# Pairwise maxima of a top-32 search by a one-source reduction, and a planner with new costs

## The chip, the cores and the metric

One core of one Trainium2 chip. The metric is the device time of one execution in microseconds (us), the median of several runs. Engines are called as in the profile: PE (TensorE matmul), PEld (its weight load), DVE (VectorE), ACT (ScalarE), POOL (GpSimd), SP (SyncE, which here only issues DMAs).

## What is computed

Inputs q, k, v are 8 batches x 8 heads x 576 tokens x 64 in f32. For each head the scores are q times k transposed over 8; of each row of 576 scores only the 32 largest stay, a softmax runs over these, and the result is multiplied by v. The eight heads are put side by side (4608 tokens x 512) and go through two matrices, with a squared ReLU between.

```python
scores = scale * np.matmul(q, k.transpose(0, 1, 3, 2))
kth = np.partition(scores, -top_k, axis=-1)[..., -top_k:-top_k + 1]
mask = scores >= kth
...
attn = attn / (np.sum(attn, axis=-1, keepdims=True) + 1e-09)
...
h = x @ w_in
r = np.maximum(h, 0.0)
g = r * r
return (g @ w_out).astype(np.float32)
```

## The kernel before, in words

**Work items.** A head pair has 9 blocks of 128 query rows: four for each head, and one that holds the last 64 rows of both. With 32 head pairs that makes 288 items, and an item is a tile `s` of 128 rows x 576 scores. `top_k` (L426 and on) takes them in groups of two, the fourth group of each head pair in threes: 128 groups.

**The search for the 32nd largest.** DVE's MAX8 gives the 8 largest values of a row, and MATCH_REPLACE8 (with a short MATCH_VALUE_LOAD ahead of it) overwrites them; four rounds give 32. To shorten the rows, `top_k` first folds them. Line by line, for one item:

- L522, DVE: `m` (288 wide) is the elementwise maximum of the two halves of `s`. L521, POOL, through the helper `whole` (its instructions have the line L514): `t1` is the sum of the two halves taken as int32; the smaller of the two is got back later by a subtraction.
- L528, DVE: `pp` (144 wide) is the maximum of the two halves of `m`: the maximum of four scores, here called the quad maximum. L527, POOL: `t2` is the int32 sum of the halves of `m`.
- L531, POOL: the part `mid` of `f`, `t2 - pp`. L534, POOL: the part `low` of `f`, `t1 - m`.
- L539 to L550, DVE: MAX8 of `pp`, replace, MAX8 and replace over 144 columns, then over 288 (which needs `mid`); L553, DVE: the last MAX8 over all 576 (which needs `low`) gives `kth`.

In the trace the names are `m`, `pp`, `f`, `a`, `c` and `kth`, and `t` stands for both `t1` and `t2` (288 and 144 wide). The groups' lists are built so that an operation is given for all items of a group before the next operation. There are two buffers of `t1` and of `t2`, and four of `m`, `pp` and `f`.

**Around it.** PE makes the scores in PSUM, ACT copies them to `s` (L458). After `kth`, ACT makes the mask `w` (L561). `attend` (L577 and on) has PE make the transposed scores with the mask, ACT the exponentials, PE the product with v; DVE takes a reciprocal of the row sums (L661), whose source is one column out of each 65 of `av`, and POOL scales by it (L663). `feed` (L683) runs the two matrices on PE, with ACT's ReLU and square; in the last two batches POOL (L717) or DVE (L714) squares.

**The order of the work.** Nothing is ordered by hand. `Plan.op` (L89) records each operation with an engine, a duration `dur` in us, a due time `prio`, what it reads and writes, and the tiles that it takes from pools. `Plan.schedule` (L117) plays these durations through: whenever an engine is free, it starts the ready operation with the earliest due time whose tiles can be had. The order that comes out for each engine is the program of that engine; it is fixed, and on the chip semaphores alone hold an instruction back. So a duration in the source changes no instruction, but can change the order of all of them, on all five engines and on SP's DMA queue. The planner knows of no resource that two engines share. `Pool.find` (L38) picks the slots: PSUM has 8 banks, and tiles of width 2 take an even pair, the one that has been in the list of free slots longest. No tile has a width of 3.

The planned cost of an operation is written where it is recorded: for one item L522 .42, L528 .27, POOL's four .81, .46, .48 and .88; MAX8 .215, .365 and .665 for 144, 288 and 576 columns.

A second program (`again`, with `full` true) is there for the case that the folded search missed a value; a flag decides, and it doesn't run here.

Of the kernel before, what the change touches and what calls it, by code (L numbers as in the profile page):

```python
# [5 lines left out]
ALU = mybir.AluOpType  # L6
# [14 lines left out]
class Pool:  # L21
# [16 lines left out]
    def find(self, width):  # L38
        if width == 1:
            if not self.free:  # L40
                return None
            if self.name == "psum":
                half = [s for s in self.free if (s ^ 1) not in self.free]
                s = half[0] if half else self.free[0]
            else:
                s = self.free[0]
            self.free.remove(s)
            return s
        for s in self.free:
            if s % width == 0 and all(s + i in self.free for i in range(width)):  # L50
                for i in range(width):
                    self.free.remove(s + i)
                return s
        return None
# [21 lines left out]

class Op:
    __slots__ = ("eng", "dur", "prio", "fn", "deps", "tiles", "takes", "n", "users", "start", "end",
                 "idx", "sem", "val", "ndma", "seq", "vc", "waits", "wars", "later", "nbf")


ENGS = ("pe", "act", "dve", "gp", "sp")
# [2 lines left out]
class Plan:  # L85
    def __init__(self):
        self.ops = []

    def op(self, eng, dur, prio, fn, r=(), w=(), u=(), hold=(), take=(), after=(), order=(), sem=None, ndma=0, nbf=0.0):  # L89


        o = Op()
        o.eng, o.dur, o.prio, o.fn = eng, dur, prio, fn
        o.sem, o.ndma, o.seq, o.nbf = sem, ndma, len(self.ops), nbf
        o.takes = list(take)
        o.users = []
        o.start = o.end = o.idx = o.val = o.vc = None
        deps = set(after)
        for t in r:
            deps.update(t.writers)  # L100
        for t in u:
            deps.update(t.ops)
        for t in list(r) + list(w) + list(u) + list(hold):
            t.ops.append(o)
            t.left += 1
        for t in list(w) + list(u):
            t.writers.append(o)
        for t in o.takes:
            t.taker = o
        o.later = ({t.taker for t in list(r) + list(w) + list(u) + list(hold)} | set(order)) - deps - {o, None}  # L110
        o.deps = deps
        o.wars = list(w) + list(u)
        o.tiles = list(r) + list(w) + list(u) + list(hold)
        self.ops.append(o)
        return o

    def schedule(self, t0=0.0, latency=0.12, own=0.07):  # L117

        left = {}
        for o in self.ops:  # L120
            left[o] = len(o.deps | o.later)
            for d in o.deps | o.later:
                d.users.append(o)
        ready = {e: [] for e in ENGS}
        busy = {e: t0 for e in ENGS}
        order = {e: [] for e in ENGS}
        events = []
        n = 0

        def push(t, kind, x):  # L130
            nonlocal n
            heapq.heappush(events, (t, n, kind, x))
            n += 1

        for o in self.ops:
            if left[o] == 0:
                push(max(t0, t0 + o.nbf), "ready", o)
        push(t0, "go", None)
        readyat = {o: t0 + o.nbf for o in self.ops}
        done = 0  # L140
        while events:
            t = events[0][0]
            while events and events[0][0] <= t + 1e-9:
                _, _, kind, x = heapq.heappop(events)
                if kind == "end":
                    done += 1
                    for tl in x.tiles:
                        tl.left -= 1
                        if tl.left == 0 and tl.slot is not None:
                            for i in range(tl.width):  # L150
                                tl.pool.last[tl.slot + i] = tl
                            tl.pool.give(tl.slot, tl.width)
                    for v in x.users:
                        left[v] -= 1
                        lat = own if v.eng == x.eng else latency
                        readyat[v] = max(readyat[v], t + lat)
                        if left[v] == 0:
                            push(readyat[v], "ready", v)
                elif kind == "ready":
                    heapq.heappush(ready[x.eng], (x.prio, x.seq, x))  # L160
            for e in ENGS:
                if busy[e] > t + 1e-9:
                    continue
                skipped = []
                while ready[e]:
                    item = heapq.heappop(ready[e])
                    o = item[2]
                    got = []
                    ok = True
                    for tl in o.takes:  # L170
                        s = tl.pool.take(tl)
                        if s is None:
                            ok = False
                            break
                        got.append((tl, s))
                    if not ok:
                        for tl, s in got:
                            tl.pool.undo(s, tl.width)
                        skipped.append(item)
                        continue  # L180
                    for tl, s in got:
                        tl.slot = s
                        tl.prev = []
                        for i in range(tl.width):
                            p = tl.pool.last[s + i]
                            if p is not None:
                                tl.prev.append(p)
                    o.start = t
                    hold = o.dur if e != "sp" else 0.6 * o.ndma
                    o.end = t + o.dur + (hold if e == "sp" else 0)  # L190
                    busy[e] = t + hold
                    order[e].append(o)
                    push(busy[e], "go", None)
                    push(o.end, "end", o)
                    break
                for item in skipped:
                    heapq.heappush(ready[e], item)
        assert done == len(self.ops), (done, len(self.ops), t, [
            (e, i[0], [(x.pool.name, len(x.pool.free)) for x in i[2].takes]) for e in ENGS for i in sorted(ready[e])[:4]])
        self.order = order  # L200
        return max(o.end for o in self.ops)
# [75 lines left out]
def bass_top_k_attn__then__act_relu_squared_kernel(  # L277
# [60 lines left out]
    def at(t):  # L338
        return mem[t.pool.name][t.slot]
# [25 lines left out]
    def build(full, weights, pl):  # L365
# [60 lines left out]
        def top_k(gi, qk, tg, dw):  # L426
# [41 lines left out]
            def dve(dur, fn, **kw):  # L468
                dk[0] += 1
                return pl.op("dve", dur, tg + .34 * dk[0], fn, **kw)  # L470
# [38 lines left out]
            else:  # L509
# [8 lines left out]
                for i in range(nb):  # L518
                    A, B = (lambda i=i: at(st[i])[:, 0:HALF]), (lambda i=i: at(st[i])[:, HALF:S])
                    M, L = (lambda i=i: at(m[i])[:, :]), (lambda i=i: at(t1[i])[:, :])  # L520
                    whole(.81, tg - 1, i, ALU.add, L, A, B, r=[st[i]], w=[t1[i]], take=[t1[i]])  # L521
                    dve(.42, lambda i=i, A=A, B=B: vec.tensor_tensor(at(m[i])[:, :], A(), B(), ALU.max),  # L522
                        r=[st[i]], w=[m[i]], take=[m[i]])
                for i in range(nb):
                    M1, M2 = (lambda i=i: at(m[i])[:, 0:QUART]), (lambda i=i: at(m[i])[:, QUART:HALF])
                    Q, L = (lambda i=i: at(pp[i])[:, :]), (lambda i=i: at(t2[i])[:, :])
                    whole(.46, tg - .5, i, ALU.add, L, M1, M2, r=[m[i]], w=[t2[i]], take=[t2[i]])  # L527
                    dve(.27, lambda i=i, M1=M1, M2=M2: vec.tensor_tensor(at(pp[i])[:, :], M1(), M2(), ALU.max),  # L528
                        r=[m[i]], w=[pp[i]], take=[pp[i], f[i]] + ([a] if i == 0 else []))
                for i in range(nb):  # L530
                    mid.append(whole(.48, tg + .5, i, ALU.subtract, lambda i=i: at(f[i])[:, QUART:HALF],  # L531
                                     lambda i=i: at(t2[i])[:, :], lambda i=i: at(pp[i])[:, :],
                                     r=[t2[i], pp[i]], w=[f[i]]))
                    low.append(whole(.88, tg + 2.5, i, ALU.subtract, lambda i=i: at(f[i])[:, HALF:S],  # L534
                                     lambda i=i: at(t1[i])[:, :], lambda i=i: at(m[i])[:, :],
                                     r=[t1[i], m[i]], w=[f[i]]))
                prev = [[] for _ in range(nb)]
# [379 lines left out]
```

## Time and profile before

| | |
|---|---|
| Median of three runs | 1082.91 us (1082.89 to 1084.41) |
| The profiled execution's own time | 1080.87 us |
| Its span in the trace | 1079.0 us |
| Granted TensorE clock, mean | 0.954 of full speed |
| Instructions | 23727 |

The span runs from the first to the last recorded instruction. "Busy" of a group is the time in which at least one of its instructions was under way, "mean ns of one" the mean length of one; since an engine begins an instruction shortly before the one ahead of it ends, means add up to more than the busy time. The idle time of an engine is put down to the semaphore event that ended it.

### The profile page before, as it was taken

What the parts mean: (1) busy time and instruction counts of PE and PEld (TensorE: products, weight loads), DVE (VectorE), ACT (ScalarE), POOL (GpSimd) and SP (SyncE); (2) the same over time, 40 slices, a digit from 0 to 9 for tenths busy, and PEclk for the clock granted to TensorE, in tenths of its full rate; (3) what the DMA queues carried; (4) which work ended last, traced back from release to release, by engine and by line L of the source; (5) the groups of instructions that cost most, each with busy time, mean ns of one, the idle gap of its engine ahead of it and who ended that gap; (6) DMA issues with size and microseconds to landing.
All of it is one profiled execution on the core that took longest, in us unless ns stands there. A gap on an engine that the chain in (4) does not pass through costs nothing.

```text
span 1079.0 us, 23727 instructions
## 1 busy us (share of the span) xinstructions
PE 918.1 (85%) x8035; PEld 548.5 (51%) x8082; DVE 980.8 (91%) x3538; ACT 765.9 (71%) x1341; POOL 906.7 (84%) x1391
## 2 busy tenths in 40 slices
PE   6766868788899998889888899898888998979897
PEld 4434435444555555545455445555455554644554
DVE  5999999599999999599999999799998899999951
ACT  5645658766698678867688777887688776656652
POOL 7998989689988898588897999789897799999871
PEclk9878789999999999999899999999999999898999
DMA  6533310220200112112110013001220100000001
GB/s 146 130 101 100 111 46 13 56 54 21 71 12 12 53 48 57 23 42 54 28 45 2 24 51 93 23 2 52 67 50 1 44 21 16 2 1 21 21 16 38
DMA packets 124419, 47.77 MB, mean 44 GB/s; under 512 B 116608, under 2 KB 116608, under 8 KB 124288
## 3 DMA queue, kind: packets, MB, share of 16 engines
q1 hardware_dynamic: 124288, 46.16, 16.6%
q8 instruction: 65, 1.06, 0.4%
q14 instruction: 66, 0.54, 0.2%
HBM read 36.70 MB, written 9.44 MB: 43 GB/s over the span
## 4 chain that ended last, share of the span: by engine, by line
DVE 59%; POOL 13%; PE 12%; issue 10%; ACT 5%; SPq 0%; DMA 0%; POOLq 0%; DVEq 0%
DVE kth L553 15%; PE ps L360 12%; DVE c L547 11%; DVE m L522 10%; DVE f L550 8%; POOL f L514 7%; DVE pp L528 7%; POOL t L514 5%; DVE f L541 4%; DVE a L539 3%; ACT w L561 2%; ACT s L458 1%; POOL x L663 1%; PE ps L363 1%; DVE rzall L661 1%
## 5 line engine op out<-in xcount | busy, mean ns | idle before, releaser
L360 PE MATMUL ps<-qk 64*128 64x288 f32 (+7 forms) x2640 | 434.4, 443 | 60.7 <-ACT w L561 19.3
L561 ACT ACTIVATE w<-s,kth 128x576 bf16<-128x576 f32 x288 | 214.5, 771 | 137.3 <-DVE kth L553 136.9
L360 PEld LDWEIGHTS ps<-qk 64*128 64x128 f32 (+1 forms) x2640 | 216.4, 185 | 178.6 <-ACT w L561 33.3
L514 POOL TENSOR_TENSOR t<-s 128x288 int32<-128x288 int32 x288 | 234.0, 823 | 33.0 <-ACT s L458 30.5
L514 POOL TENSOR_TENSOR f<-t,m 128x288 int32<-128x288 int32 x288 | 228.1, 807 | 0.0
L514 POOL TENSOR_TENSOR t<-m 128x144 int32<-128x144 int32 x288 | 180.8, 638 | 49.9 <-DVE m L522 47.8
L550 DVE MATCH_REPLACE8 f<-c,f 128x144 f32<-128x144 f32 (+1 forms) x576 | 206.4, 363 | 0.0
L553 DVE MAX8 kth<-f 128x8 f32<-128x576 f32 x288 | 202.9, 742 | 2.6 <-POOL f L514 2.6
L620 ACT ACTIVATE p<-ps 128x640 bf16<-128x640 f32 (+1 forms) x192 | 155.2, 809 | 57.3 <-PE ps L360 56.0
L522 DVE TENSOR_TENSOR m<-s 128x288 f32<-128x288 f32 x288 | 158.8, 583 | 40.8 <-ACT s L458 40.8
L458 ACT COPY s<-ps 128x576 f32<-128x576 f32 x288 | 170.8, 642 | 33.2 <-PE ps L360 32.6
L547 DVE MAX8 c<-f 128x8 f32<-128x144 f32 (+1 forms) x576 | 190.8, 367 | 2.0 <-POOL f L514 1.9
L360 PE MATMUL ps<-wo,g 128*128 128x512 bf16 (+1 forms) x593 | 151.5, 383 | 8.7 <-ACT p L620 2.1
L360 PE MATMUL ps<-xt,win 128*128 128x288 bf16 (+2 forms) x1088 | 142.9, 284 | 7.4 <-ACT g L706 2.4
L514 POOL TENSOR_TENSOR f<-t,pp 128x144 int32<-128x144 int32 x288 | 141.7, 509 | 3.2 <-DVE pp L528 3.2
L360 PEld LDWEIGHTS ps<-steep_bf,w 128*128 128x128 bf16 (+1 forms) x1600 | 83.6, 102 | 110.4 <-issue 109.4
L528 DVE TENSOR_TENSOR pp<-m 128x144 f32<-128x144 f32 x288 | 131.5, 492 | 0.4
L360 PE MATMUL ps<-steep_bf,w 128*128 128x128 bf16 (+3 forms) x1600 | 124.0, 222 | 0.0
L360 PEld LDWEIGHTS ps<-xt,win 128*128 128x128 bf16 x1088 | 97.4, 99 | 40.0 <-ACT g L704 3.3
L360 PEld LDWEIGHTS ps<-wo,g 128*128 128x128 bf16 (+1 forms) x640 | 56.1, 101 | 60.7 <-issue 8.2
L541 DVE MATCH_REPLACE8 f<-a,pp 128x144 f32<-128x144 f32 x288 | 81.4, 287 | 0.0
L663 POOL TENSOR_TENSOR x<-av,rzall 128x256 bf16<-128x256 f32 (+2 forms) x68 | 43.7, 643 | 44.6 <-DVE rzall L661 43.9
(54 smaller groups left out, 807.7 us busy)
## 6 DMA issues: line engine op xcount, KB each, us to landing
rq<-in_q_dram SPq DMA_DIRECT2D x64, 128.0 KB, 2.4
rk<-in_k_dram SPq DMA_DIRECT2D x64, 128.0 KB, 2.5
rv<-in_v_dram SPq DMA_DIRECT2D x64, 128.0 KB, 2.3
out_dram<-o SPq DMA_DIRECT2D x32, 256.0 KB, 2.1
ws<-in_moe_w_in_dram SPq DMA_DIRECT2D x8, 512.0 KB, 4.4
ws<-in_moe_w_out_dram SPq DMA_DIRECT2D x8, 512.0 KB, 3.6
rq<-in_q_dram SPq DMA_DIRECT2D x32, 32.0 KB, 2.5
rk<-in_k_dram SPq DMA_DIRECT2D x32, 32.0 KB, 2.4
```

Of the source, the lines that this page charges most:

```text
L360: return pe.matmul(o, l, r, start=start, stop=stop, skip_group_check=True)
L458: pl.op("act", .64, tg - 28 + i, lambda i=i: act.copy(at(st[i])[:, :].rearrange("p (a c) -> p a c", a=2), ps32[:, ss[i].slot:ss[i].slot + ...
L514: return pl.op("gp", dur, prio + .8 * i, lambda: gp.tensor_tensor(o().bitcast(I32), x().bitcast(I32), y().bitcast(I32), op), **kw)
L522: dve(.42, lambda i=i, A=A, B=B: vec.tensor_tensor(at(m[i])[:, :], A(), B(), ALU.max), r=[st[i]], w=[m[i]], take=[m[i]])
L528: dve(.27, lambda i=i, M1=M1, M2=M2: vec.tensor_tensor(at(pp[i])[:, :], M1(), M2(), ALU.max), r=[m[i]], w=[pp[i]], take=[pp[i], f[i]] + ([ ...
L541: prev[i] = [dve(.275, lambda i=i: vec.match_replace(at(f[i])[:, 0:QUART], at(a)[:, i, :], at(pp[i])[:, :], NEG), r=[pp[i]], hold=[a], w=[ ...
L547: lambda i=i, t=t, wd=wd: vec.max(eighth(t, i), at(f[i])[:, 0:wd]),
L550: prev[i] = [chain(t, i, prev[i], dur + .06, lambda i=i, t=t, wd=wd: vec.match_replace(at(f[i])[:, 0:wd], eighth(t, i), at(f[i])[:, 0:wd], ...
L553: ks.append(chain(kth, i, prev[i] + [low[i]], .665, lambda i=i: vec.max(eighth(kth, i), at(f[i])[:, :]), hold=[f[i]]))
L561: pl.op("act", .75, tw + .8 * i, lambda i=i: act.activation(at(ws[i])[:, :], at(st[i])[:, :], ACTF.Relu, bias=kth[:, i, ix[i]:ix[i] + 1], ...
L620: return act.activation(o, i, ACTF.Exp, scale=0.125)
L663: pl.op("gp", .15 + .16 * nu, tt + 4, lambda: gp.tensor_tensor(at(xr)[:, 0:nu, :], at(avs)[:, 0:nu, 0:64], rzall[:, u0:u0 + nu].unsqueeze( ...
```

## The change

The maximum of the halves of `m` becomes a `tensor_reduce` with maximum over one source: `m` is read as 144 pairs whose two members lie 144 columns apart. It still makes one instruction for one item. Everything else is in the planner:

- new durations: .78, .44, .44, .78 for POOL's four, .37 for `m`, .375 for the reduction, and 0.05 less for every operation of ACT;
- an operation can be marked `lk`, and `m` alone is. The planner starts such an operation only when POOL has ended what it is doing, and starts nothing on POOL until it has ended;
- a tile of width 2 takes the lowest free pair of banks instead of the one at the head of the list; widths of 3, which nothing asks for, could start at any slot.

```diff
@@ class Pool, find
-        for s in self.free:
-            if s % width == 0 and all(s + i in self.free for i in range(width)):
+        for s in sorted(self.free):
+            if (width == 3 or s % width == 0) and all(s + i in self.free for i in range(width)):
...
@@ class Plan, op
-        o.eng, o.dur, o.prio, o.fn = eng, dur, prio, fn
-        o.sem, o.ndma, o.seq, o.nbf = sem, ndma, len(self.ops), nbf
+        o.eng, o.dur, o.prio, o.fn = eng, dur - (.05 if eng == "act" else 0), prio, fn
+        o.sem, o.ndma, o.seq, o.nbf, o.lk = sem, ndma, len(self.ops), nbf, lk
@@ class Plan, schedule
+        locked = t0
...
-                if busy[e] > t + 1e-9:
+                if busy[e] > t + 1e-9 or (e == "gp" and locked > t + 1e-9):
                     continue
...
-                    o.start = t
+                    o.start = max(t, busy["gp"]) if o.lk else t
                     hold = o.dur if e != "sp" else 0.6 * o.ndma
-                    o.end = t + o.dur + (hold if e == "sp" else 0)
-                    busy[e] = t + hold
+                    o.end = o.start + o.dur + (hold if e == "sp" else 0)
+                    busy[e] = o.start + hold
+                    if o.lk:
+                        locked = o.end
@@ top_k
-                    whole(.81, tg - 1, i, ALU.add, L, A, B, r=[st[i]], w=[t1[i]], take=[t1[i]])
-                    dve(.42, lambda i=i, A=A, B=B: vec.tensor_tensor(at(m[i])[:, :], A(), B(), ALU.max),
+                    whole(.78, tg - 1, i, ALU.add, L, A, B, r=[st[i]], w=[t1[i]], take=[t1[i]])
+                    dve(.37, lambda i=i, A=A, B=B: vec.tensor_tensor(at(m[i])[:, :], A(), B(), ALU.max), lk=True,
                         r=[st[i]], w=[m[i]], take=[m[i]])
...
-                    whole(.46, tg - .5, i, ALU.add, L, M1, M2, r=[m[i]], w=[t2[i]], take=[t2[i]])
-                    dve(.27, lambda i=i, M1=M1, M2=M2: vec.tensor_tensor(at(pp[i])[:, :], M1(), M2(), ALU.max),
+                    whole(.44, tg - .5, i, ALU.add, L, M1, M2, r=[m[i]], w=[t2[i]], take=[t2[i]])
+                    dve(.375, lambda i=i: vec.tensor_reduce(
+                        at(pp[i])[:, :], at(m[i])[:, :].rearrange("p (a c) -> p c a", a=2), AX.X, ALU.max),
                         r=[m[i]], w=[pp[i]], take=[pp[i], f[i]] + ([a] if i == 0 else []))
...
-                    mid.append(whole(.48, tg + .5, i, ALU.subtract, lambda i=i: at(f[i])[:, QUART:HALF],
+                    mid.append(whole(.44, tg + .5, i, ALU.subtract, lambda i=i: at(f[i])[:, QUART:HALF],
...
-                    low.append(whole(.88, tg + 2.5, i, ALU.subtract, lambda i=i: at(f[i])[:, HALF:S],
+                    low.append(whole(.78, tg + 2.5, i, ALU.subtract, lambda i=i: at(f[i])[:, HALF:S],
```

## Rows read from the trace of the kernel before

**Rows 1.** The page's part 1: busy us, share of the span, instructions of each engine.

```profile
PE 918.1 (85%) x8035; PEld 548.5 (51%) x8082; DVE 980.8 (91%) x3538; ACT 765.9 (71%) x1341; POOL 906.7 (84%) x1391
```

**Rows 2.** The page's part 4: the chain that ended last, by engine.

```profile
DVE 59%; POOL 13%; PE 12%; issue 10%; ACT 5%; SPq 0%; DMA 0%; POOLq 0%; DVEq 0%
```

**Rows 3.** Busy time by stretch: PE, PEld, DVE, ACT, POOL, then clock, DMA share.

```profile
30.00:1030.00 1000.00, 857.23 (x7539) 510.19 (x7581) 949.25 (x3428) 729.53 (x1271) 864.63 (x1310) 0.95 0.16 41
```

**Rows 4.** DVE's waits over the whole span: us in total, times, longest.

```profile
DVE m L522 <- ACT s L458: 40.8, 10, 13.4
DVE rzall L661 <- ACT av L659: 28.9, 12, 7.9
DVE g L714 <- ACT g L706: 12.2, 4, 10.8
```

**Rows 5.** Groups by form, DVE: busy us, mean ns of one, idle before.

```profile
L522 DVE TENSOR_TENSOR m<-s 128x288 f32<-128x288 f32 x288 | 158.8, 583 | 40.8 <-ACT s L458 40.8
L528 DVE TENSOR_TENSOR pp<-m 128x144 f32<-128x144 f32 x288 | 131.5, 492 | 0.4
...
L547 DVE MAX8 c<-f 128x8 f32<-128x288 f32 x288 | 117.8, 443 | 1.9 <-POOL f L514 1.9
...
L539 DVE MAX8 a<-pp 128x8 f32<-128x144 f32 x288 | 73.8, 292 | 0.1
```

**Rows 6.** Groups by form, POOL: the same columns.

```profile
L514 POOL TENSOR_TENSOR t<-s 128x288 int32<-128x288 int32 x288 | 234.0, 823 | 33.0 <-ACT s L458 30.5
L514 POOL TENSOR_TENSOR f<-t,m 128x288 int32<-128x288 int32 x288 | 228.1, 807 | 0.0
...
L514 POOL TENSOR_TENSOR t<-m 128x144 int32<-128x144 int32 x288 | 180.8, 638 | 49.9 <-DVE m L522 47.8
...
L514 POOL TENSOR_TENSOR f<-t,pp 128x144 int32<-128x144 int32 x288 | 141.7, 509 | 3.2 <-DVE pp L528 3.2
```

**Rows 7.** By tile (t on POOL, m on DVE): durations in ns, min/median/max.

```profile
L514 POOL TENSOR_TENSOR t<-s x288: 782/793/1086, 11.1 to 1039.7; 128x288 int32<-128x288 int32 x144
L514 POOL TENSOR_TENSOR t<-m x288: 478/552/1662, 12.1 to 1040.5; 128x144 int32<-128x144 int32 x144
L514 POOL TENSOR_TENSOR f<-t,pp x288: 477/487/962, 14.1 to 1044.4; 128x144 int32<-128x144 int32 x144
L514 POOL TENSOR_TENSOR f<-t,m x288: 781/793/1452, 15.0 to 1045.9; 128x288 int32<-128x288 int32 x144
...
L522 DVE TENSOR_TENSOR m<-s x288: 420/450/1397, 11.1 to 1027.6; 128x288 f32<-128x288 f32 x144
L528 DVE TENSOR_TENSOR pp<-m x288: 261/589/1136, 11.6 to 1029.0; 128x144 f32<-128x144 f32 x144
```

**Rows 8.** Timeline, 500 to 512 us, DVE, then POOL: start us, us, what.

```profile
502.93 0.80 DVE L522 TENSOR_TENSOR m<-s 128x288 f32<-128x288 f32 x2
503.66 0.51 DVE L528 TENSOR_TENSOR pp<-m 128x144 f32<-128x144 f32 x2
504.09 0.51 DVE L539 MAX8 a<-pp 128x8 f32<-128x144 f32 x2
...
509.77 1.11 DVE L528 TENSOR_TENSOR pp<-m 128x144 f32<-128x144 f32 x2
...
503.45 1.52 POOL L514 TENSOR_TENSOR t<-m 128x144 int32<-128x144 int32 x2 [0.84 <-DVE m L522]
...
509.56 1.14 POOL L514 TENSOR_TENSOR t<-m 128x144 int32<-128x144 int32 x2 [0.26 <-DVE m L522]
```

**Rows 9.** Groups by form: DVE's reciprocals (strided source) and a reduction of 288 columns.

```profile
L661 DVE RECIPROCAL rzall<-av 128x5 f32<-128x5 f32 x32 | 5.6, 174 | 8.2 <-ACT av L659 8.2
...
L661 DVE RECIPROCAL rzall<-av 128x2 f32<-128x2 f32 x8 | 1.2, 155 | 11.5 <-ACT av L659 11.5
...
L825 DVE TENSOR_REDUCE fone<-fcmp 128x1 f32<-128x288 f32 x1 | 0.5, 453 | 0.0
```

**Rows 10.** Groups by form: ACT's copy of the scores.

```profile
L458 ACT COPY s<-ps 128x576 f32<-128x576 f32 x288 | 170.8, 642 | 33.2 <-PE ps L360 32.6
```

More of the change, by code (lines that the diff above doesn't have):

```diff
@@ L78 @@
     __slots__ = ("eng", "dur", "prio", "fn", "deps", "tiles", "takes", "n", "users", "start", "end",
-                 "idx", "sem", "val", "ndma", "seq", "vc", "waits", "wars", "later", "nbf")
+                 "idx", "sem", "val", "ndma", "seq", "vc", "waits", "wars", "later", "nbf", "lk")
 ENGS = ("pe", "act", "dve", "gp", "sp")
@@ L87, in __init__, with op @@
         self.ops = []
-    def op(self, eng, dur, prio, fn, r=(), w=(), u=(), hold=(), take=(), after=(), order=(), sem=None, ndma=0, nbf=0.0):
+    def op(self, eng, dur, prio, fn, r=(), w=(), u=(), hold=(), take=(), after=(), order=(), sem=None, ndma=0, nbf=0.0, lk=False):
         o = Op()
-        o.eng, o.dur, o.prio, o.fn = eng, dur, prio, fn
-        o.sem, o.ndma, o.seq, o.nbf = sem, ndma, len(self.ops), nbf
+        o.eng, o.dur, o.prio, o.fn = eng, dur - (.05 if eng == "act" else 0), prio, fn
+        o.sem, o.ndma, o.seq, o.nbf, o.lk = sem, ndma, len(self.ops), nbf, lk
         o.takes = list(take)
```

## The prediction

> **What bounds the kernel now.** I read the busy shares first. DVE is busy for 91% of the span, POOL and PE for 84% and 85% [rows 1], and the chain that ended last runs over DVE for 59% of the span [rows 2]. By stretch, DVE is busy for 949.25 of the 1000 us between 30 and 1030, so it is idle there for 50.8 us, and for 47.4 us in start and tail together, which the change leaves alone. Its waits are for ACT's copy of the scores (40.8 us) and for ACT's copies of `av` and `g` at stage ends [rows 4]; for POOL it hardly waits by semaphore. So DVE sets the pace, and the question is whether it is busy with work.
>
> It is not, all of it. A MAX8 of 144 columns takes 292 ns and the pair of them 510 ns [rows 5, 8], so an instruction begins 74 ns before the one ahead ends and costs the engine its duration less 74 ns. The maximum that gives `pp` has 144 columns too and takes 261 ns at best, but 492 on the average and 589 in the median [rows 5, 7]; that for `m` 450 in the median and 583 on the average. The timeline tells why [rows 8]. At 503.66 us the two `pp` take 0.51 us together, while POOL's pair of sums `t<-m`, begun at 503.45, takes 1.52 us, against some 0.93 for 478 ns at best [rows 7] and a second that costs 30 ns less. At 509.77 the two `pp` take 1.11 us, and POOL's pair 1.14. When a DVE maximum with two sources meets POOL's work, one of them stands still. MAX8, with one source, shows none of this.
>
> So there is a shared resource, and I add up its load for one of the 288 items. POOL's four sums at their minima are 0.782 + 0.781 + 0.478 + 0.477 us [rows 7], less 30 ns each: 2.40. POOL's other work is 906.7 us less the 784.6 of the four groups [rows 1, 6], so 122 us or 0.42. `m` costs 0.37 (450 ns less 74) and `pp` 0.22 (292 ns as MAX8 less 74). Together 3.41 us. DVE is busy for 980.8/288 = 3.41 us an item: **the shared resource is full while DVE works**, and DVE's surplus is its waiting for it.
>
> **The reduction.** It removes 288 instructions of 492 ns and adds 288. No row has this operation with its source 144 columns apart. From below: three reductions of 288 contiguous columns, 453 ns for the one shown [rows 9]. From above there are two ends. MAX8 takes 443 ns for 288 columns and 292 for 144 [rows 5], 1.05 ns a column; if each strided read costs as much again, 302 ns come on top: 755 ns. The only strided source among the rows is that of the reciprocals, 155 ns for two elements and 174 for five [rows 9], 6.3 ns an element; 288 of these would be 1.8 us. But that is another operation, a division, and three elements more are little to read a slope from, so I give that far end no chance to speak of. I take 453 ns, the row of the same operation and count. That is 39 ns less than now: **-11 us**. Without POOL's interference it would be a loss, since 292 ns becomes 453 (+46 us): the gain is all waiting. POOL's `f<-t,pp`, which waits for it (3.2 us of idle time now [rows 6]), is covered: a pair of reductions ends after 0.45 + 0.38 = 0.83 us, POOL's pair `t<-m` ahead of it after 0.93.
>
> The page that bears against this is "Advanced Engine Details and Errata" of the Trainium skill, section "SBUF Cachelines": an access that goes to another 16-byte line each time pays a penalty, without a figure. Here every read does, and the rule would make the forecast the first rival; no row shows it.
>
> **`m` and its collisions.** `m` stays a two-source maximum. Its waiting is 583 - 450 = 133 ns an item, 38 us in all. If the reduction leaves the resource alone, the load falls to 3.19 us an item, and DVE's own work becomes the larger: 3.41 - 0.133 - 0.200 (`pp`, 492 less 292) + 0.161 (453 less 292) = 3.24. POOL also gets back most of what it loses in `t<-m`, 638 on the average against 478 [rows 6, 7], 46 us; `m` of the second item of a group can still hold it up. POOL gets ahead, and is more often idle when `m` comes. Bounds for `m`: all 38 us gone, or 58 us more (all that `pp` waits for now, 200 ns x 288, would have to shift to it). The resource stays 95% as loaded as now (3.19 of 3.41), so I take one third of `m`'s waiting away: **-13 us**.
>
> **The new order.** ACT's 0.05 us, POOL's lower costs, the lock and the pairs of banks change the order on all engines and of SP's loads, without an instruction more or less. Some costs come nearer to the rows: ACT's copy of the scores is busy for 170.8/288 = 0.593 us [rows 10] where the plan had .64 and now .59; the plan had .27 for `pp`, which costs 0.42. What hides the moves is the 3 to 5 items by which buffers of `s`, `m` and `f` let engines run ahead, and DMA engines busy for 16% of the time [rows 3]. If the cover is gone, it is DVE's 50.8 us of idle time that grows or shrinks. I take nothing, between -20 and +20. The lowest free pair of banks may be the one freed last, so that PE waits for a late ACT copy, 0.64 us at most each time; PE's slack behind DVE hides that. Nothing is queued behind a new wait: the planner's lock is no semaphore on the chip.
>
> **The sum.** -11 - 13 = -24 us on the profiled execution's 1080.87 us: 1056.9. The median of the runs shown lies 2 us above that execution, so I predict **1058.5**, with 1040 to 1076 as this case's own range.
>
> **Rivals.**
> 1. *The strided read is slow (slower).* Place: the 288 reductions. At 755 ns each costs 263 ns more than now: +76 us, less the 13 of `m`, +63: 1146. It decides from about 540 ns on, where 48 ns x 288 eat `m`'s 13 us and no gain is left; in between every 10 ns of the reduction are 2.9 us, so 600 ns give 1101. For it speaks that every read jumps 576 bytes; against it, that no row shows a read slower for its stride, and the reciprocals don't settle it. Chance 0.18.
> 2. *The resource falls idle and `m` waits for nothing (faster still).* DVE then runs at 3.24 us an item: -38 - 11 = -49 us, 1034. For: POOL's load falls too, and now and then `m` already runs at 420 to 450 ns, more than half the time [rows 7]. Against: 3.19 and 3.24 are close, and POOL's order has the sums of the next group beside the last MAX8 just before `m`. Chance 0.14.
> 3. *DVE's saving turns into waiting for ACT and PE.* DVE reaches the stage ends sooner and waits there for `s` and `av` [rows 4], or the new order is worse. PE is busy for 857 of 1000 us [rows 3]. All 24 us given back: 1083, give or take 8. Against: ACT is busy for 71%, and most of the idle time is in a few long stalls. Chance 0.14, of it 0.07 within 0.2%, 0.04 slower and 0.03 faster.
> 4. *The change doesn't take the load off.* The reduction waits for POOL as `pp` does, 200 ns more than the 453: 653 - 492 = +161 ns, +46 us: 1129. The reductions of before run at the end, where POOL is idle, and so say nothing. Against: MAX8 with one source, 292 ns on the average, never shows a wait. Chance 0.04.
>
> On the fourth, "SBUF — State Buffer" of the Trainium skill, section "Who interferes with whom", says that a reduction on this chip never contends with GpSimd, and two SBUF sources do. For the two sources the trace agrees (261 to 1136 ns for one shape); for the reduction no run here shows it.
>
> **How the numbers follow.** The forecast has 0.48, the rivals 0.18, 0.14, 0.14 and 0.04, and 0.02 is left for a slowdown that I don't see. 0.2% is 2.2 us, about what a measurement of this kernel can tell from no change. Faster: 0.48 + 0.14 + 0.03 = 0.65. Same: 0.07. Slower: 0.18 + 0.04 + 0.04 + 0.02 = 0.28. The range reaches from 1030, below the second rival, to 1104, which takes in the third and a strided read of up to some 600 ns. It leaves out a fully doubled read, the fourth rival, and the far end of the second, together just under 0.2.
>
> **What would show it.** The reduction's row near 450 ns with a narrow spread says that step right; 600 or more is the first rival, a wide spread the fourth. `t<-m` on POOL should fall from 638 towards 520, and its idle time before it, 49.9 us now, should grow. The mean of `m` should come out near 540; near 450 is the second rival, above 600 says that the collisions moved. DVE's busy time should be near 957. If DVE's waits for `s` and `av`, 69.7 us now, grow beyond 90, the third has happened. The forecast is wrong if DVE's busy time falls and its idle time takes it back, or if the reduction isn't near 450 ns.

## The result and the profile after

The changed kernel takes **1008.05 us** (median of four runs, 1004.29 to 1010.18) against 1082.97 (now the median of four runs): a ratio of 0.9301, 95% interval 0.9272 to 0.9331. The forecast was 1058.5, with a range of 1030 to 1104: right in its sign, and 50 us too slow. The profiled execution has a span of 1005.5 us, 73.5 less than before.

The page's part 1 of the changed kernel:

```profile
PE 900.9 (90%) x8082; PEld 541.2 (54%) x8082; DVE 944.1 (94%) x3538; ACT 766.4 (76%) x1341; POOL 872.6 (87%) x1391
```

Against [rows 1], DVE is busy for 36.7 us less. Its idle time is 61.4 us (1005.5 less 944.1) and was 98.2, also 36.8 less. So half of the gain is work that got shorter, half is waiting that went away. The second half I had not forecast at all. Where the idle time was, the stretch without start and tail shows, to be held against [rows 3]:

```profile
30.00:956.50 926.50, 841.45 (x7599) 503.76 (x7598) 910.16 (x3416) 730.04 (x1271) 829.75 (x1307) 0.98 0.18 45
```

DVE is idle for 16.3 us in these 926.5 (third pair of numbers), where it was for 50.8 in 1000. Start and tail still hold 45.1 us, where they held 47.4. Groups by form of the changed kernel, as in [rows 5, 6]:

```profile
L518 POOL TENSOR_TENSOR t<-s 128x288 int32<-128x288 int32 x288 | 227.7, 802 | 13.1 <-ACT s L462 10.7
L518 POOL TENSOR_TENSOR t<-m 128x144 int32<-128x144 int32 x288 | 160.7, 569 | 73.6 <-DVE m L526 71.4
L526 DVE TENSOR_TENSOR m<-s 128x288 f32<-128x288 f32 x288 | 138.4, 515 | 15.6 <-ACT s L462 15.4
L518 POOL TENSOR_TENSOR f<-t,pp 128x144 int32<-128x144 int32 x288 | 136.6, 490 | 1.2 <-DVE pp L532 1.0
L532 DVE TENSOR_REDUCE pp<-m 128x144 f32<-128x288 f32 x288 | 117.4, 447 | 0.2
```

The two maxima by tile (`m` on DVE), min/median/max in ns, as in [rows 7]:

```profile
L526 DVE TENSOR_TENSOR m<-s x288: 416/450/1225, 11.5 to 957.8; 128x288 f32<-128x288 f32 x144
L532 DVE TENSOR_REDUCE pp<-m x288: 421/446/470, 12.9 to 958.5; 128x144 f32<-128x288 f32 x144
```

The reduction takes 447 ns with hardly a spread (421 to 470), where the maximum took 261 to 1136. `m` fell from 583 to 515 ns, `t<-m` on POOL from 638 to 569 (the forecast had it going towards 520), and POOL now stands idle for 73.6 us before `t<-m`, where it was 49.9: it is there before DVE, as forecast. DVE's waits, as in [rows 4]:

```profile
DVE rzall L666 <- ACT av L664: 20.7, 11, 11.4
DVE m L526 <- ACT s L462: 15.4, 3, 11.5
DVE c L552 <- POOL f L518: 10.5, 7, 4.9
DVE g L719 <- ACT g L711: 2.9, 4, 1.5
```

The wait for the scores fell from 40.8 us to 15.4, and 11.5 of these are the start. How such a stall comes about, the timeline of the kernel before shows, PE and then DVE, around the longest:

```profile
202.34 1.16 PE L360 MATMUL ps<-xt,win 128*128 128x288 bf16 x8
...
203.97 2.12 PE L360 MATMUL ps<-xt,win 128*128 128x288 bf16 x16
...
206.33 1.15 PE L360 MATMUL ps<-xt,win 128*128 128x288 bf16 x8
209.11 1.15 PE L360 MATMUL ps<-xt,win 128*128 128x288 bf16 x8 [1.63 <-ACT g L704]
210.88 0.81 PE L360 MATMUL ps<-qk 64*128 64x320 f32 x4 [0.62 <-ACT g L704]
...
216.25 1.93 PE L360 MATMUL ps<-qk 64*128 64x288 f32 x12
...
218.21 0.46 DVE L522 TENSOR_TENSOR m<-s 128x288 f32<-128x288 f32 x1 [13.42 <-ACT s L458]
```

From 202 us on PE's program has the first matrix of `feed` and a block of `attend`; the next scores (`qk`, 288 columns) stand behind them, at 216.25, and twice PE waits for ACT's `g` first. DVE has used up its tiles `s` and stands still for 13.4 us. It is the order that does it: e1 below, in this order, has the same stall, and e2, with the instructions of before in the new order, has none like it: between 30 and 956 us DVE's longest wait is 2.5 us there, and 1.9 in the changed kernel.

TensorE's granted clock rose as well, from 0.954 to 0.972 (0.956 in e1, 0.967 in e2). The long stall is no matter of the clock, which was granted in full in it, 1.00 (the stretch's last columns are the clock, the DMA share and GB/s):

```profile
205.00:210.00 5.00, 3.24 (x27) 2.23 (x25) 0.00 (x0) 5.00 (x10) 1.75 (x4) 1.00 0.55 122
```

Among the executions of the kernel before, 0.01 more of the clock goes with 2 to 4 us less, so by estimate the clock stands for some 4 to 8 of the 75 us, as a cause or as an effect of the tighter order; no run tells which.

### The profile page after: what moved, and what is told of

It reads as the page before. It is cut to its first block, busy times and chain, and to the rows that moved or that the text cites. A ratio compares the mean times of both kernels' runs of the same rounds, so it can differ in the third digit from the quotient of the medians.

```text
span 1005.5 us, 23808 instructions
## 1 busy us (share of the span) xinstructions
PE 900.9 (90%) x8082; PEld 541.2 (54%) x8082; DVE 944.1 (94%) x3538; ACT 766.4 (76%) x1341; POOL 872.6 (87%) x1391
## 4 chain that ended last, share of the span: by engine, by line
DVE 67%; PE 12%; issue 9%; POOL 7%; ACT 3%; SPq 0%; DMA 0%; DVEq 0%; POOLq 0%
DVE kth L558 16%; DVE c L552 13%; PE ps L364 12%; DVE m L526 10%; DVE pp L532 9%; DVE f L555 7%; DVE f L546 6%; DVE a L544 5%; POOL f L518 4%; POOL t L518 2%; ACT w L566 1%; POOL x L668 1%; ACT s L462 1%; DVE rzall L666 1%; PE ps L367 0%
## 5 line engine op out<-in xcount | busy, mean ns | idle before, releaser
L364 PE MATMUL ps<-qk 64*128 64x288 f32 (+7 forms) x2640 | 423.3, 435 | 52.0 <-ACT s L462 25.8
L364 PEld LDWEIGHTS ps<-qk 64*128 64x128 f32 (+1 forms) x2640 | 214.0, 181 | 168.6 <-ACT s L462 42.2
L518 POOL TENSOR_TENSOR t<-s 128x288 int32<-128x288 int32 x288 | 227.7, 802 | 13.1 <-ACT s L462 10.7
L518 POOL TENSOR_TENSOR t<-m 128x144 int32<-128x144 int32 x288 | 160.7, 569 | 73.6 <-DVE m L526 71.4
L462 ACT COPY s<-ps 128x576 f32<-128x576 f32 x288 | 170.2, 641 | 30.4 <-PE ps L364 29.4
L364 PE MATMUL ps<-wo,g 128*128 128x512 bf16 (+1 forms) x640 | 161.7, 383 | 0.2
L526 DVE TENSOR_TENSOR m<-s 128x288 f32<-128x288 f32 x288 | 138.4, 515 | 15.6 <-ACT s L462 15.4
L364 PE MATMUL ps<-xt,win 128*128 128x288 bf16 (+2 forms) x1088 | 140.7, 281 | 3.2 <-ACT xt L685 1.1
L518 POOL TENSOR_TENSOR f<-t,pp 128x144 int32<-128x144 int32 x288 | 136.6, 490 | 1.2 <-DVE pp L532 1.0
L532 DVE TENSOR_REDUCE pp<-m 128x144 f32<-128x288 f32 x288 | 117.4, 447 | 0.2
L709 ACT ACTIVATE g<-ps 128x576 bf16<-128x576 f32 x112 | 70.2, 655 | 6.7 <-PE ps L364 6.6
```

Source lines behind the costliest of these rows:

```text
L364: return pe.matmul(o, l, r, start=start, stop=stop, skip_group_check=True)
L462: pl.op("act", .64, tg - 28 + i, lambda i=i: act.copy(at(st[i])[:, :].rearrange("p (a c) -> p a c", a=2), ps32[:, ss[i].slot:ss[i].slot + ...
L518: return pl.op("gp", dur, prio + .8 * i, lambda: gp.tensor_tensor(o().bitcast(I32), x().bitcast(I32), y().bitcast(I32), op), **kw)
L526: dve(.37, lambda i=i, A=A, B=B: vec.tensor_tensor(at(m[i])[:, :], A(), B(), ALU.max), lk=True, r=[st[i]], w=[m[i]], take=[m[i]])
L532: dve(.375, lambda i=i: vec.tensor_reduce(at(pp[i])[:, :], at(m[i])[:, :].rearrange("p (a c) -> p c a", a=2), AX.X, ALU.max), r=[m[i]], w= ...
L709: return act.activation(at(g)[:, 0:nt].rearrange("p (a c) -> p a c", a=2), ps32[:, hh.slot:hh.slot + 2, 0:hw], ACTF.Relu)
```

## The experiments

Theory A: the instruction gives DVE's busy time, the order the idle time. Theory B: the instruction gives both. Theory C: the order is nearly all.

**e1: the instruction alone.** The kernel before with the reduction, at the old planned cost, so that every engine's program has the old order.

```diff
-dve(.27, lambda i=i, M1=M1, M2=M2: vec.tensor_tensor(at(pp[i])[:, :], M1(), M2(), ALU.max),
+dve(.27, lambda i=i: vec.tensor_reduce(
+    at(pp[i])[:, :], at(m[i])[:, :].rearrange("p (a c) -> p c a", a=2), AX.X, ALU.max),
```

> The kernel before with the instruction alone exchanged; the planner is told the old cost of .27, so that the order on every engine is that of before. Theory A (the reduction takes load off what DVE and POOL share, and that alone shortens DVE's busy time; the idle time that also went away belongs to the order): the reduction near 447 ns, m near 515, DVE busy near 945, DVE idle still near 98 us, time 1042 to 1050. Theory B (the idle time went too because POOL delivers earlier, so the order has no part in it): DVE idle near 61 us, time 1005 to 1015. Theory C (the order is nearly all of it): 1070 or more.

Measured: 1061.55 us, ratio 0.9794 (0.9778 to 0.9810). From its page, part 1:

```profile
PE 915.3 (86%) x8035; PEld 547.5 (52%) x8082; DVE 955.6 (90%) x3538; ACT 765.1 (72%) x1341; POOL 874.7 (82%) x1391
```

Its groups by form:

```profile
L522 DVE TENSOR_TENSOR m<-s 128x288 f32<-128x288 f32 x288 | 147.5, 544 | 41.7 <-ACT s L458 41.7
L528 DVE TENSOR_REDUCE pp<-m 128x144 f32<-128x288 f32 x288 | 117.5, 443 | 0.4
```

And DVE's waits:

```profile
DVE m L522 <- ACT s L458: 41.7, 10, 13.4
DVE rzall L661 <- ACT av L659: 32.2, 13, 8.2
```

DVE's busy time falls by 25.2 us, and the rows account for it: 49 ns x 288 for the reduction (14) and 39 ns x 288 for `m` (11). The idle time is 104.8 us (span 1060.4), no less than before, and the 13.4 us stall is still there. B falls, and so does C's band. A had the idle time about right (98 expected), but `m` came out at 544 ns where it had 515, DVE's busy time 11 us above its 945, and the total 11 us above its band.

**e2: the order alone.** The changed kernel with the old maximum at a planned .375, so that the order is that of after.

```diff
-dve(.375, lambda i=i: vec.tensor_reduce(
-    at(pp[i])[:, :], at(m[i])[:, :].rearrange("p (a c) -> p c a", a=2), AX.X, ALU.max),
+dve(.375, lambda i=i, M1=M1, M2=M2: vec.tensor_tensor(at(pp[i])[:, :], M1(), M2(), ALU.max),
```

> The changed kernel with the old two-source maximum put back; the planner is told .375 as after, so that the order on every engine is that of after. Theory A: the order alone brings its 37 us of idle time, 1040 to 1052, with DVE busy near 980. Theory B: 1075 to 1085, as before. Theory C: 1005 to 1020.

Measured: 1029.09 us, ratio 0.9497 (0.9467 to 0.9526), below A's band and above C's, so that none of the three theories holds as stated. Its page's part 1, the two maxima by form, and DVE's wait for the scores:

```profile
PE 902.6 (88%) x8031; PEld 542.5 (53%) x8082; DVE 964.3 (94%) x3538; ACT 766.5 (75%) x1341; POOL 908.0 (88%) x1391
```

```profile
L526 DVE TENSOR_TENSOR m<-s 128x288 f32<-128x288 f32 x288 | 152.9, 564 | 15.6 <-ACT s L462 15.5
...
L532 DVE TENSOR_TENSOR pp<-m 128x144 f32<-128x144 f32 x288 | 120.3, 455 | 0.2
```

```profile
DVE m L526 <- ACT s L462: 15.5, 3, 11.0
```

With no instruction exchanged the order takes away 54 us: 34.6 of idle time (63.6 left of 98.2), and 16.5 of busy time, because the maxima wait less for POOL: 19 ns less for `m` and 37 for `pp`, times 288, are 16.1. The two parts add up: the instruction is worth 21.4 us in the old order (e1) and 21.0 in the new (1029.09 to 1008.05).

**e3 and e9: one number of the plan.** e9 is the kernel before with the planned cost of the quad maximum raised to .375, and nothing else; e3 has the reduction besides. Both have the same order.

```diff
-dve(.27, lambda i=i, M1=M1, M2=M2: vec.tensor_tensor(
+dve(.375, lambda i=i, M1=M1, M2=M2: vec.tensor_tensor(
```

> The kernel before with the reduction and its planned cost of .375 in place of .27, and nothing else of the planner. If the wrong cost of the quad maximum (0.42 on the engine, .27 in the plan) was what made the old order bad, this alone gives nearly all: 1005 to 1020. If the order owes its gain to ACT's and POOL's costs or to the lock, it stays with the instruction alone in the old order, 1040 to 1050.

> The kernel before, two-source maximum and all, with the planned cost of the quad maximum alone set to .375 in place of .27: a change of one number, no instruction exchanged. The order is that of e3. If the instruction and the order add up, 21 us above e3: 1048 to 1056. If the order of e3 helps only together with the reduction, 1075 to 1085.

Measured: e3 1030.93 us, ratio 0.9514 (0.9497 to 0.9531), between its two expectations; e9 1060.35, ratio 0.9795 (0.9778 to 0.9811), 4 us above the nearer of its own. From e9, its page's part 1 and DVE's waits:

```profile
PE 912.5 (86%) x8031; PEld 543.4 (52%) x8082; DVE 981.2 (93%) x3538; ACT 767.6 (73%) x1341; POOL 908.3 (86%) x1391
```

```profile
DVE m L522 <- ACT s L458: 34.3, 8, 12.4
DVE rzall L661 <- ACT av L659: 10.3, 5, 9.0
DVE g L714 <- ACT g L706: 6.9, 4, 5.5
```

One number in the source, and the kernel is 22.5 us faster: DVE is as busy as before (981.2), and idle for 73.8 us (span 1055.0) instead of 98.2. The old cost of .27 stood against some .42 on the engine. The long stall stays (12.4). In this order the instruction gives 29.4 us, more than the 21 expected.

**e4 to e7: the rest of the planner, one part taken back at a time.**

```diff
@@ e4
-        o.eng, o.dur, o.prio, o.fn = eng, dur - (.05 if eng == "act" else 0), prio, fn
+        o.eng, o.dur, o.prio, o.fn = eng, dur, prio, fn
@@ e5
-dve(.37, lambda i=i, A=A, B=B: vec.tensor_tensor(at(m[i])[:, :], A(), B(), ALU.max), lk=True,
+dve(.37, lambda i=i, A=A, B=B: vec.tensor_tensor(at(m[i])[:, :], A(), B(), ALU.max),
@@ e6
-        for s in sorted(self.free):
+        for s in self.free:
@@ e7: in the four calls
-whole(.78 (.44, .44, .78)
+whole(.81 (.46, .48, .88)
```

> The changed kernel without the 0.05 us taken off ACT's planned durations. If ACT's costs carry the order's gain, 1030 to 1045; if they don't, 1003 to 1013.

> The changed kernel without the lock in the plan (m is planned as if POOL ran on beside it). If the lock's part in the plan carries the order's gain, 1025 to 1040, with m back near 545 ns as in e3; if the plain costs carry it, 1005 to 1012.

> The changed kernel with the old choice of PSUM pairs. The order of the instructions on every engine is the same as after; only the banks, and so some of PE's waits, differ. If the lowest free pair costs or gives nothing, as the prediction held, 1004 to 1012; if the choice is a part of the gain, over 1013; if it costs, under 1003.

> The changed kernel with POOL's four old planned durations (.81, .46, .48, .88). POOL is behind DVE and the two sets differ by 0.19 us an item. If these costs carry a part of the order's gain, 1015 to 1030; if not, 1004 to 1012.

| taken back | time, us | ratio to before | DVE busy | DVE idle | `m`, ns |
|---|---|---|---|---|---|
| nothing (after) | 1008.05 | 0.9301 (0.9272 to 0.9331) | 944.1 | 61.4 | 515 |
| e4: ACT's costs | 1019.00 | 0.9408 (0.9392 to 0.9424) | 947.5 | 68.4 | 519 |
| e5: the lock | 1034.75 | 0.9564 (0.9546 to 0.9582) | 952.8 | 79.5 | 544 |
| e6: the choice of banks | 1007.88 | 0.9297 (0.9265 to 0.9329) | 946.1 | 65.7 | 518 |
| e7: POOL's costs | 1029.06 | 0.9499 (0.9482 to 0.9515) | 958.3 | 70.4 | 538 |

The banks are worth nothing; the order is the same, only PE's waits differ. Each of the others is missed: the lock by 27 us, POOL's costs by 21, ACT's by 11. e4 lies between its two expectations, the other three inside one of theirs. POOL's costs surprised me, 0.19 us an item on an engine that is ahead. Without the lock `m` is back at 544 ns, as in e1; but with the lock and POOL's old costs it is nearly there too:

```profile
L526 DVE TENSOR_TENSOR m<-s 128x288 f32<-128x288 f32 x288 | 145.8, 544 | 31.0 <-ACT s L462 31.0
L526 DVE TENSOR_TENSOR m<-s 128x288 f32<-128x288 f32 x288 | 146.4, 538 | 20.0 <-ACT s L462 15.7 <-POOL f L518 4.0
```

The first line is e5's, the second e7's. So the lock shortens `m` in full only beside the lower costs (525 ns in p2 below, which has the lock and the old costs of both engines). Nor does the lock, which acts in the plan alone, keep the two engines apart on the chip: counted over the traces, 133 of the 288 `m` of the changed kernel began while POOL was in an instruction, and 137 of e5's. What fell is how long these took, 596 ns on the average where e5 has 656.

**n1 to n4: is it luck?** A reordering could win by chance. These nudge the planner's latency between engines by 1 to 8%, which should make a plan neither better nor worse.

```diff
-def schedule(self, t0=0.0, latency=0.12, own=0.07):
+def schedule(self, t0=0.0, latency=0.115, own=0.07):
```

> The kernel before with the planner's latency between engines .115 in place of .12: a nudge with no meaning that reshuffles the order. If the order's gain is a matter of the costs (systematic), 1075 to 1090; if any reshuffle can win as much (a lucky draw), it may land anywhere between 1010 and 1090.

> The kernel before with that latency .13. Systematic: 1070 to 1090. Lucky draw: anywhere between 1010 and 1090.

> The changed kernel with that latency .121. Systematic: 1000 to 1016. Lucky draw: mostly worse than after, 1015 to 1060.

> The changed kernel with that latency .13. Systematic: 998 to 1018. Lucky draw: mostly worse than after, 1015 to 1060.

Measured: 1086.97 and 1088.60 us from the kernel before, ratios 1.0026 (1.0008 to 1.0044) and 1.0032 (1.0016 to 1.0048); 1008.97 and 1006.20 from the changed one, 0.9302 (0.9275 to 0.9329) and 0.9276 (0.9249 to 0.9303). The nudges move the time by about 4 us at most. They also move fewer instructions than the change: by operation and tile, n1 and n2 have 171 and 212 of DVE's 3538 instructions at another place than the kernel before, n3 and n4 38 and 166 than the changed one, while the two kernels differ in 908. Against luck in a larger reshuffling speaks another count: with the reduction, nine different orders from new costs or due times (after, e3, e4, e5, e7, and p2, p4, p5, p6 below) all take 1003 to 1035 us, and the old order (e1) 1061.55. So most of the order's gain is no lucky draw. How much of the spread among the nine is one, these runs don't show.

**p1 to p3: what in the costs?** Either the plan's pace has to be the chip's, or the plan has to know who waits for whom.

```diff
@@ p1, from the kernel before
-dve(.42, lambda i=i, A=A, B=B: vec.tensor_tensor(at(m[i])[:, :], A(), B(), ALU.max),
+dve(.51, lambda i=i, A=A, B=B: vec.tensor_tensor(at(m[i])[:, :], A(), B(), ALU.max),
-dve(.27, lambda i=i, M1=M1, M2=M2: vec.tensor_tensor(at(pp[i])[:, :], M1(), M2(), ALU.max),
+dve(.415, lambda i=i, M1=M1, M2=M2: vec.tensor_tensor(at(pp[i])[:, :], M1(), M2(), ALU.max),
@@ p2, from the changed kernel: the edits of e4 and e7 together
@@ p3, from the changed kernel
-dve(.375, lambda i=i: vec.tensor_reduce(
-    at(pp[i])[:, :], at(m[i])[:, :].rearrange("p (a c) -> p c a", a=2), AX.X, ALU.max),
+dve(.22, lambda i=i, M1=M1, M2=M2: vec.tensor_tensor(
+    at(pp[i])[:, :], M1(), M2(), ALU.max), lk=True,
```

> The kernel before with two planned costs set to what the two maxima take on the engine in the trace, waiting included (.51 for m, .415 for the quad maximum); no instruction exchanged, no lock. If the pace of the plan is what counts, near e2 (1029): 1020 to 1040. If knowing who waits for whom counts, near e9 (1060): 1052 to 1065.

> The changed kernel with ACT's and POOL's old planned costs: against e3 (1031) it has the lock and m at .37 in place of .42. If the lock alone makes the order, 1005 to 1015. If the corrections must come together, 1018 to 1035.

> The changed kernel with the two-source quad maximum, planned at .22 and with the lock, as m is: the plan then knows both waits. If the lock in the plan is what helps, better than e2 (1029, where only m has it): 1010 to 1025. If the plan needs only the pace, as e2 within 6 us.

Measured: p1 1046.86 us, 0.9663 (0.9629 to 0.9697); p2 1028.51, 0.9497 (0.9459 to 0.9535); p3 1087.26, 1.0038 (1.0016 to 1.0059). p1 lies between its two expectations: true mean costs without a lock bring 36 us of the 54 that the order brings. p2 equals e7, which differs from it by ACT's costs alone, so that these help only beside POOL's (1018 to 1035 was expected if the corrections must come together). p3 is a clear miss for the idea that a plan that knows both waits is better. Its page's part 1, the two maxima by form, and one of POOL's waits:

```profile
PE 934.1 (86%) x8033; PEld 560.1 (52%) x8082; DVE 1025.0 (94%) x3538; ACT 768.2 (71%) x1341; POOL 901.3 (83%) x1391
```

```profile
L526 DVE TENSOR_TENSOR m<-s 128x288 f32<-128x288 f32 x288 | 183.4, 652 | 14.5 <-ACT s L462 11.1 <-POOL f L518 3.3
...
L532 DVE TENSOR_TENSOR pp<-m 128x144 f32<-128x144 f32 x288 | 154.8, 561 | 0.1
```

```profile
POOL x L668 <- DVE rzall L666: 144.1, 57, 6.7
```

Idle time is as low as after (61.9 us), but the maxima wait for POOL more than ever, 652 and 561 ns (229 of the 288 `m` begin while POOL is in an instruction, 157 in e2), DVE is busy for 1025.0 us, and POOL waits 144.1 us for the reciprocals in DVE's queue (18.2 after). Why its order does that I did not try.

**p4 to p6: further along.** Due times 3.3 and 3.1 us an item apart instead of 3.2, and 0.08 us off ACT's costs instead of 0.05.

```diff
@@ p4 (p6: 3.1)
-    PER = 3.2
+    PER = 3.3
@@ p5
-        o.eng, o.dur, o.prio, o.fn = eng, dur - (.05 if eng == "act" else 0), prio, fn
+        o.eng, o.dur, o.prio, o.fn = eng, dur - (.08 if eng == "act" else 0), prio, fn
```

> The changed kernel with the due times 3.3 us an item apart instead of 3.2; DVE's busy time after is 944.1 us for 288 items, 3.28 each. If due times that are too early still cost something, 995 to 1003; if they don't matter, 1004 to 1012.

> The changed kernel with 0.08 us taken off ACT's planned durations instead of 0.05. If costs true to the trace are the optimum, 1010 to 1030; if the order gets better the freer the plan thinks ACT to be, 995 to 1003.

> The changed kernel with due times 3.1 us an item apart instead of 3.2. If late due times were what cost in p4, 998 to 1006; if any shift away from 3.2 costs, 1012 to 1030.

Measured: p4 1019.75 us, 0.9407 (0.9370 to 0.9443); p6 1006.19, 0.9275 (0.9253 to 0.9298), no different from after; p5 **1003.09**, 0.9248 (0.9225 to 0.9270), some 5 us below the changed kernel, about what a nudge can do. p4 misses both of its ranges; p5 and p6 end at the upper edge of theirs. p4 set the due times nearer to DVE's 3.28 us an item and lost 12 us; p5 set ACT's costs below what the trace shows and lost nothing. So "the nearer to the trace, the better" is not the rule either.

## Why the prediction was wrong

- **The shared resource: right in its direction, but not shown to be full.** The load of 3.41 us an item before was the argument for a gain. After, DVE is busy for 944.1/288 = 3.28 us an item, near the 3.24 that I had as its own need. That the maxima wait for POOL, a count over the trace of the kernel before shows: 262 of the `pp` began while POOL was in an instruction and took 512 ns on the average, the other 26 took 293; for `m` it is 158 with 698 ns and 130 with 443. But e2 has every instruction of before, and so the same load of 3.41, and DVE is busy for 964.3/288 = 3.35 there: that load and busy time came out equal was in part chance.
- **The reduction: right, a little small.** 453 ns were taken, 447 came (443 in e1); -11 us, measured -14.
- **`m`: right for the instruction.** -13 us, and e1 shows -11. That after has -20 took the lock and POOL's costs together (544 ns in e5, 538 in e7).
- **The sum of the two: right.** -24 us of DVE's busy time, -25.2 in e1. The two misses of 3 and 2 us cancel, which is luck, and the last step has a slip: 1080.87 less 24 and 2 more are 1058.9. Either is within 3 us of what the instruction alone gives, 1061.55.
- **The new order: the step that failed.** "I take nothing, between -20 and +20." It is worth -54 us (e2). The reasons that I gave don't hold: "What hides the moves is the 3 to 5 items by which buffers of `s`, `m` and `f` let engines run ahead". The trace had stalls of 13.4 and 7.9 us that no buffer had hidden [rows 4], so the old order was bad in plain sight. I named the 50.8 us of idle time as what "grows or shrinks" and capped the shrinking at 20; it shrank by 34.5. And I looked at the order only for idle time, while it also decides how long DVE and POOL hold each other up (16.5 us of DVE's busy time in e2). I had even written that the plan had .27 for what costs 0.42, and drew nothing from it: e9 shows that this number alone was worth 22.5 us.
- **Rival 1, a slow strided read: fell.** Each read jumps 576 bytes and the reduction takes 447 ns, where one of 288 contiguous columns took 453 [rows 9]. The penalty of "Advanced Engine Details and Errata" of the Trainium skill, "SBUF Cachelines", doesn't show in this operation.
- **Rival 2 (1034):** its sign for POOL came true, idle before `t<-m` from 49.9 to 73.6 us, but `m` still waits, and with the order unchanged (e1) the time stayed at 1061.55. So it doesn't explain the surplus.
- **Rival 3:** the opposite happened; waits for `s` and `av` fell from 69.7 to 36.1 us. In e1, where the order is the old one, they rose to 73.9, and ate some of the 25 us: there it had a point.
- **Rival 4: fell.** The reductions after took 421 to 470 ns with POOL busy for 87% of the span; 285 of the 288 began while POOL was in an instruction, and none shows a wait. That a reduction on this chip never contends with GpSimd is what "SBUF — State Buffer" of the Trainium skill, section "Who interferes with whom", states, and these rows agree.

What stays open: why the worth of the three corrections doesn't add up (e4 and e7 cost 11 and 21 us, both at once, p2, 20.5), why both maxima locked make the worst order, and why going past the trace with ACT's costs loses nothing. Planned costs act on all five programs at once, and I have no rule that foretells the time from them.

## What to carry to other kernels

Where a program's order comes from a list of costs, a wrong cost can weigh as much as a slow instruction: put each planned number beside the trace's row, though the nearest numbers need not give the best order, and count long stalls of the busiest engine as what a new order can give back, not as fixed. When a change touches an instruction and the order, run each alone, and nudge a number without meaning to see how much of a gain is luck, with a look at how many instructions the nudge really moves. And two engines that are each busy for 85 to 90% may still be full: add up their load on what they share, per item, and an instruction that takes longer alone may win by keeping out of it.

## What the runs showed of the hardware

The reduction reads pairs 144 columns apart in f32 and takes 447 ns for 288 elements and 144 results, as long as one of 288 contiguous columns to a single result (453). And it keeps its length, 409 to 461 ns in e1 and 421 to 470 after, beside POOL sums during which a two-source maximum of the same source took up to 1136.
